# A ConvNeXt V2 block on one core: the slot's conv in two stretches, seven gelu tiles, and work moved between ScalarE, VectorE, GpSimd and TensorE

## The chip, the core and the metric

The kernel runs on one core of a Trainium2 chip. The engines are named as in the profile: PE (TensorE, with its weight loads as PEld), ACT (ScalarE), DVE (VectorE), POOL (GpSimd) and SP (SyncE, which here only issues transfers). Each has a queue of its own that it works off in order. The metric is device time in microseconds (us). Before the change it was 1480.13 us, the median of 3 runs (1479.71 to 1490.58). A difference under about 1% (14.8 us) is treated as one that a measurement of this kernel can't tell from none.

## What is computed

```python
def reference(x, dw, w1, w2, grn_gamma, grn_beta):   # x: 1 x 512 x 512 x 96, bf16
    xp = jnp.pad(x, ((0,0),(1,1),(1,1),(0,0)))
    out = sum(xp[:, i:i+H, j:j+W, :] * dw[i, j] for i in range(3) for j in range(3))
    h = (out - mean(out)) / sqrt(var(out) + 1e-5)      # over the 96 channels
    h = gelu(einsum('bhwc,ce->bhwe', h, w1))           # 96 -> 384, tanh approximation
    gx = sqrt((h * h).sum(axis=(1, 2)) + 1e-6)         # over the whole image
    nx = gx / (gx.mean(axis=-1) + 1e-6)
    h = grn_gamma * (h * nx) + grn_beta + h
    return x + einsum('bhwe,ec->bhwc', h, w2)
```

The sum `gx` runs over the whole image, so nothing can be written before all of `h` has been seen once.

## The kernel before, in words

The image is cut into 128 blocks of 4 rows (2048 pixels). A first pass computes the conv, the norm, the first matrix product and gelu for each block, and from the gelu output only the 384 sums of squares; a few blocks' gelu outputs are kept. A second pass, about the last third of the time, loads or recomputes `h`, multiplies it with `w2` (scaled by the sums) and adds `x`. The change is in the first pass.

The first pass is a loop over slots `s` (line 831). A table `at` (lines 799 to 825) says which block's step of which kind falls into which slot, and within a slot the order of the calls is the order in each engine's queue (`InOrder`). A block `b` passes through these steps:

- `load_x` (SP) and `turn_x` (DVE, two transposes of 128 x 576), three and more slots ahead of the conv.
- The conv, `conv_taps` (lines 462 to 504): 72 matmuls of 64 x 32 weights over 511 or 512 columns. `h` is the half of the array's rows (channels and rows of the input), `j` the output row (a column tile of 32), `i` one of the three PSUM banks of `Y3` (banks 4 to 6), `dx` the horizontal shift; eight tiles (two `h` times four `j`) work side by side. It goes in three bursts of 24 (`taps[0]` to `taps[2]`). In burst `n` the half `h` writes bank `(n + h) % 3`, so that the two halves never write one bank at the same time; `pe.drain()` keeps bursts apart where nothing else lies between.
- `evac`: ACT copies the three banks to `y_bf` (128 x 1536, bf16) in one instruction.
- `stage_sq` one slot later: POOL squares `y_bf`. `stage_stats` two slots after the conv: 24 matmuls with four columns add up `y` and `y * y` over the channels in bank 7 (`S`), up to 64 columns for each of the two sums in a batch of four blocks.
- For a batch: `stage_moments` (DVE: `S / C` from PSUM, then a memset of `S`), one slot later `stage_rstd` (POOL: variance and the integer guess of its inverse root, four small ops), then `stage_newton` (POOL, eight), `stage_turn` (DVE), `stage_rows` and `stage_bcast` (SP, through DRAM). Then for each block `stage_norm` (POOL: `yn = y * rstd`), `stage_write` and `stage_read` (SP, through DRAM), which gives `ynT`.
- `mlp_units(b)`, 14 slots after the conv in the long middle stage: the matrix product with `w1p` in PSUM and gelu on ACT. The block has 12 banks of product. `unit(bank, n)` makes `n` of them and one gelu over them; `banks(2)` gives banks 0 and 1, `banks(1)` banks 2 and 3 in turn. There are nine units: three of two banks and six of one.

The sums of squares come by two ways. A block has four quarters of 512 pixels. For the first `cm_quads(b)` of them (channels on the partitions) DVE runs `bn_stats`, three per quarter (`entry`, called by `squares` and `squares_rest`; the last three of a whole block are owed to the next slot). For the others (pixels on the partitions) PE adds up a Gram matrix, `gram_next(n)`, `n` groups of 6 matmuls of 128 x 128; a quarter is two groups, and groups wait in the list `grams`. Whole blocks (`q % 10` in 0, 3, 7: kept in DRAM for the second pass) have four quarters on DVE, three residues of ten have two, and the other four have three: 90 `bn_stats` and 20 groups in ten slots. The `g` tiles have five buffers.

A slot that has both a conv and an MLP block runs, in this order (lines 895 to 928): `conv(0)`, units 0 and 2, `squares(0)`, `conv(1)`, `turn_x`, units 3 and 4, `squares(1)`, a Gram group, units 6 and 7, `squares(2)`, `turn`, `conv(2)`, `evac`, a Gram group, units 8 and 10, stats, unit 11, moments, the rest of the squares. Slots 18 to 127 are of this kind. Before them slots with a conv alone fill the pipeline, and 14 slots with an MLP block alone (`mlp_tail`) follow.

Of the kernel before, what the change touches and what calls it, by code (L numbers as in the profile page):

```python
# [8 lines left out]
ALU = mybir.AluOpType  # L9
ACTF = mybir.ActivationFunctionType  # L10
AX = mybir.AxisListType

GR = 4
LN_EPS = 1e-5
# [3 lines left out]
BATCH = 4  # L18
NHELD = 5
WHOLE = (0, 3, 7)  # L20
NTAIL = 14
GRB = 3


class InOrder:
# [31 lines left out]
def kernel(  # L57
# [11 lines left out]
    f32 = mybir.dt.float32  # L69
# [30 lines left out]
    def cm_quads(q):  # L100
        if is_whole(q) or is_held(q):
            return NQ
        if q > HELD[0]:
            return 1
        return 2 if q >= NBLK - 16 or (q - 1) % 10 in WHOLE else 3

    whole = [q for q in range(NBLK) if is_whole(q)]
    g_dram = dram.tile([len(whole), 128, NQ * NCH * QW], bf16, name="g_dram")
# [76 lines left out]
    with ExitStack() as p1:  # L185
# [4 lines left out]
        def banks(n):  # L190
            if n == 2:
                return PS[:, 0:2, :]
            ones[0] += 1
            return PS[:, 2 + ones[0] % 2:3 + ones[0] % 2, :]
# [205 lines left out]
        n = 0  # L400
# [61 lines left out]
        def conv_taps(b, spare):  # L462
            if spare:
                Ua, Ub = banks(2), banks(1)
                Y = [Ua[:, 0, :], Ua[:, 1, :], Ub[:, 0, :]]
            else:
                Y = [Y3[:, i, :] for i in range(NI)]
            mms = []
            for n in range(3):
                mms.append([(h, j, (n + h) % NI, dx) for dx in (0, -1, 1) for j in range(GR) for h in range(2)])  # L470
            flat = [m for ms in mms for m in ms]
            first = {}
            last = {}
            for n, (h, j, i, dx) in enumerate(flat):
                first.setdefault((i, j), n)
                last[i, j] = n

            def burst(n, fence=True):
                k = sum(len(ms) for ms in mms[:n])
                for h, j, i, dx in mms[n]:  # L480
                    src = b + shift(h, j)
                    o0, o1 = max(0, -dx), W - max(0, dx)
                    pe.matmul(
                        Y[i][32 * j:32 * j + 32, o0:o1],
                        lhsT=Wq[64 * h:64 * h + 64, i, dx + 1, j, :],
                        rhs=x_rows(src, 64 * h, 64 * h + 64, i, MB * (1 + dx) + o0, o1 - o0)
                        if 0 <= src < NBLK else zrow[64 * h:64 * h + 64, o0:o1],
                        start=first[i, j] == k,
                        stop=last[i, j] == k,
                    )  # L490
                    k += 1
                if n < 2 and fence:
                    pe.drain()

            def evac():
                y = ypool.tile([128, NI, W], bf16, name="y_bf")
                if spare:
                    act.activation(out=y[:, 0:2, :], in_=Ua, func=ACTF.Identity)
                    act.activation(out=y[:, 2, :], in_=Ub[:, 0, :], func=ACTF.Identity)
                else:  # L500
                    act.activation(out=y[:], in_=Y3, func=ACTF.Identity)
                ybf[b] = y

            return [lambda fence=True, n=n: burst(n, fence) for n in range(3)], evac

        def stage_sq(b, on_act):
            q = ysqpool.tile([128, NI, W], bf16, name="ysq")
# [3 lines left out]
                pool.tensor_tensor(out=q[:], in0=ybf[b][:], in1=ybf[b][:], op=ALU.mult)  # L511
            ysq[b] = q

        def stage_stats(b):
            k = batch_of[b]
            b0, n = BATCHES[k]
            for src, h in ((ybf[b], 0), (ysq.pop(b), 1)):
                for g in range(NG):
                    c0 = (b - b0) * NG + g
                    for i in range(NI):  # L520
                        pe.matmul(S[:, h, c0:c0 + (GR - 1) * n * NG + 1:n * NG],
                                  lhsT=src[:, i, g * 128:(g + 1) * 128], rhs=rowsel[:],
                                  start=False, stop=(i == NI - 1), skip_group_check=True)


        def stage_moments(k):
            N = BATCHES[k][1] * GR * NG
            m = small.tile([128, 2, NS], f32, name="mom")
            dve.tensor_scalar(out=m[:, :, :N], in0=S[:, :, :N], scalar1=1.0 / C, scalar2=None, op0=ALU.mult)
            dve.memset(S[:], 0.0)  # L530
            msts[k] = m

        def stage_rstd(k, eng):
            N = BATCHES[k][1] * GR * NG
            m = msts.pop(k)
            var = small.tile([128, NS], f32, name="var")
            eng.tensor_tensor(out=var[:, :N], in0=m[:, 0, :N], in1=m[:, 0, :N], op=ALU.mult)
            eng.tensor_tensor(out=var[:, :N], in0=m[:, 1, :N], in1=var[:, :N], op=ALU.subtract)
            eng.tensor_scalar(out=var[:, :N], in0=var[:, :N], scalar1=0.0, scalar2=LN_EPS, op0=ALU.max, op1=ALU.add)
            ri = small.tile([128, NS], i32, name="ri")  # L540
            eng.tensor_scalar(out=ri[:, :N], in0=var[:, :N].bitcast(i32), scalar1=-0.5, scalar2=float(0x5F3759DF),
                               op0=ALU.mult, op1=ALU.add)
            rcur = ri[:, :N].bitcast(f32)
            rns[k] = (var, rcur)

        def stage_newton(k, eng):
            N = BATCHES[k][1] * GR * NG
            var, rcur = rns[k]
            for it in range(NEWTON_ITERS):
                last = it == NEWTON_ITERS - 1  # L550
                t_ = small.tile([128, NS], f32, name="nt")
                eng.tensor_tensor(out=t_[:, :N], in0=rcur, in1=rcur, op=ALU.mult)
                eng.tensor_tensor(out=t_[:, :N], in0=t_[:, :N], in1=var[:, :N], op=ALU.mult)
                eng.tensor_scalar(out=t_[:, :N], in0=t_[:, :N], scalar1=-0.5, scalar2=1.5, op0=ALU.mult, op1=ALU.add)
                rn = small.tile([128, NS], bf16 if last else f32, name="rstd" if last else "rn")
                if last and N % 32:
                    eng.memset(rn[:, N:(N + 31) // 32 * 32], 0.0)
                eng.tensor_tensor(out=rn[:, :N], in0=t_[:, :N], in1=rcur, op=ALU.mult)
                rcur = rn[:, :N]
            rns[k] = rn  # L560
# [110 lines left out]
        def mlp_tail(b, get):  # L671
# [6 lines left out]
            for t in range(NQ):  # L678
# [11 lines left out]
                        stage_stats(b2)  # L690
                if t > cm_quads(b):
                    grams.extend((b, (t - 1) * QC + k * E) for k in range(0, GR, 2))
            for k in get("moments"):
                stage_moments(k)
            if cm_quads(b) < NQ:
                grams.extend((b, (NQ - 1) * QC + k * E) for k in range(0, GR, 2))

        def mlp_units(b):
# [5 lines left out]
            def cm_mm(dst, j, t):  # L704
                pe.matmul(quad_out(dst), lhsT=w1p[:, j * 128:(j + 1) * 128], rhs=quad(yt[:], t), start=True, stop=True)

            def unit(bank, n):
                U = banks(n)
                if bank < 2 * NCH:
                    j, t0 = divmod(bank, 2)  # L710
                    for t in range(t0, t0 + n):
# [81 lines left out]
        def put(s, what, v):  # L793
            at.setdefault((s, what), []).append(v)
# [4 lines left out]
        for k, (b0, n) in enumerate(BATCHES):  # L799
# [6 lines left out]
            if ramp:  # L806
                put(last_s, "chain", k)
                put(last_s + 1, "spread", k)
            else:
                put(last_s, "moments", k)  # L810
                put(last_s + 1, "rstd", k)
                put(last_s + 2, "newton", k)
                put(last_s + 2, "turn", k)
                put(last_s + 3, "rows", k)
                put(last_s + 4, "bcast", k)
# [15 lines left out]
        for s in range(last_slot + 1):  # L831
# [15 lines left out]
                stage_sq(b, False)  # L847
            for b in get("norm"):
                stage_norm(b)
            for k in get("rstd"):  # L850
                stage_rstd(k, pool)
            mlp = get("mlp")

            def spread_out():
# [11 lines left out]
            elif not mlp:  # L866
                if s + 3 < NBLK:
                    turn_x(s + 3)
                for f in taps:
                    f()  # L870
                if not spare:
                    spread_out()
# [3 lines left out]
                    stage_sq(b, True)  # L876
                for b in get("stats"):
                    stage_stats(b)
                for k in get("moments"):
                    stage_moments(k)  # L880
                if spare:
                    spread_out()
                for k in get("chain"):
# [6 lines left out]
            else:  # L890
                b = mlp[0]
                unit, squares, squares_rest = mlp_units(b)
                conv = lambda n, fence=True: taps[n](fence) if taps else None

                conv(0)
                unit(0, 2)
                unit(2, 1)
                squares(0)
                conv(1, False)
                spread_out()  # L900
                if s + 3 < NBLK:
                    turn_x(s + 3)
                unit(3, 1)
                unit(4, 2)
                squares(1)
                gram_next(1 if taps else 2)
                unit(6, 1)
                squares(2)
                unit(7, 1)
                for k in get("turn"):  # L910
                    stage_turn(k)
                conv(2)
                if evac:
                    evac()
                gram_next(1 if taps else 2)
                unit(8, 2)
                unit(10, 1)
                for b2 in get("stats"):
                    stage_stats(b2)
                unit(11, 1)  # L920
                for k in get("moments"):
                    stage_moments(k)
                squares_rest(2)
                square_owed()
                if is_whole(b):
# [131 lines left out]
```

## Time and profile before

The profiled execution has a span of 1483.2 us; the median of the runs is 1480.13. Busy time is the share of the span in which an engine had an instruction running:

| engine | busy us | share | instructions |
|---|---|---|---|
| PE (matmul) | 1392.2 | 94% | 23125 |
| ACT | 1415.9 | 95% | 1595 |
| POOL | 1300.7 | 88% | 922 |
| DVE | 1166.9 | 79% | 2139 |

These are averages over two passes with different limits. From 300 to 900 us, inside the first pass, the largest groups are (mean length of one, which includes overlap with its neighbours):

| engine | group | count | mean ns |
|---|---|---|---|
| DVE | `bn_stats` 128x512 | 763 | 672 |
| DVE | transposes of x, f32 and bf16 | 79 each | 764 and 736 |
| ACT | gelu 128x512 | 494 | 703 |
| ACT | gelu 128x1024 | 247 | 1118 |
| ACT | `y_bf` 128x1536 | 83 | 1569 |
| POOL | `yn` 128x1536 | 85 | 3111 |
| POOL | `ysq` 128x1536 | 84 | 2754 |
| PE | `w1p` product, 512 columns | 759 | 381 |
| PE | conv, 511 or 512 columns | 5895 | 382 to 394 |
| PE | Gram 128x128 | 1059 | 220 |

In the prediction, "PE PS" and "ACT g" are a matmul into PSUM and a gelu; `g` is the gelu output, `bst` the result of `bn_stats`, `mom`, `var` and `ri` the small tiles of the variance, `o_sb` an output tile of the second pass. Line numbers in the views are those of the helper `InOrder`, so groups are told apart by their tiles.

### The profile page before, as it was taken

Reading aid. Unit: us, or ns where it says so; the run is one execution under the profiler, and the core shown is the slowest. Engines: PE = TensorE matmul, PEld = TensorE weight load, DVE = VectorE, ACT = ScalarE, POOL = GpSimd, SP = SyncE. Lnnn points to the kernel's source line nnn. Section 1 sums busy time; section 2 is a strip of 40 time slices with the busy share of each in tenths; the row PEclk is TensorE's granted clock in tenths of the full one; section 3 lists DMA queues with packets and bytes.
Section 4 is the critical chain, followed back from the end, with each engine's and each line's share of the span. In section 5 each row is a group of like instructions: output and inputs, shape, how many; then the busy total and the mean of one; then the engine's idle time right before and its main releaser. Section 6 shows DMA issues by size and latency. Waiting matters only on the chain.

```text
span 1483.2 us, 54230 instructions
## 1 busy us (share of the span) xinstructions
PE 1392.2 (94%) x23125; PEld 812.3 (55%) x23125; DVE 1166.9 (79%) x2139; ACT 1415.9 (95%) x1595; POOL 1300.7 (88%) x922
## 2 busy tenths in 40 slices
PE   8889999999999999999999997789999999999998
PEld 3334444444444444444444445467777777676766
DVE  7749989999999999999999987955555555555555
ACT  6889999999999999999999999989999999998997
POOL 3459889998999999999999996559999999999997
PEclk9999999999999999999999999999999999999999
DMA  6577788887878888888888867569999999999997
GB/s 178 166 215 235 231 245 282 250 267 243 276 240 274 258 266 259 276 248 280 265 248 264 260 217 210 188 248 404 366 352 410 415 414 413 415 408 410 401 406 279
DMA packets 167768, 433.08 MB, mean 292 GB/s; under 512 B 31558, under 2 KB 81318, under 8 KB 163046
## 3 DMA queue, kind: packets, MB, share of 16 engines
q1 hardware_dynamic: 151284, 326.04, 66.8%
q0 software_dynamic: 14880, 103.43, 17.6%
q8 instruction: 181, 2.97, 0.9%
q14 instruction: 61, 0.50, 0.1%
q10 hardware_dynamic: 1362, 0.15, 0.1%
HBM read 273.30 MB, written 156.22 MB: 290 GB/s over the span
## 4 chain that ended last, share of the span: by engine, by line
PE 31%; ACT 25%; DMA 20%; DVE 10%; POOL 8%; issue 4%; SPq 3%; ACTq 0%; POOLq 0%; DVEq 0%
PE PS L35 31%; ACT g L35 18%; DMA out_dram<-o_sb 9%; ACT y_bf L35 6%; DVE bst L35 5%; POOL yn L35 4%; DMA ynT<-yn_dram 4%; SPq L35 3%; DMA rbc<-r_dram 2%; DMA xin<-in_x_dram 2%; DVE xT L35 2%; DMA yn_dram<-yn 2%; POOL ysq L35 1%; DVE o_sb L35 1%; DMA g_dram<-g 1%
## 5 line engine op out<-in xcount | busy, mean ns | idle before, releaser
L35 ACT ACTIVATE g<-PS 128x512 bf16<-128x512 f32 (+2 forms) x1062 | 727.2, 862 | 9.3 <-PE PS L35 9.1
L35 DVE BATCH_NORM_STATS2 bst<-g 128x6 f32<-128x512 bf16 x1110 | 671.3, 673 | 29.3 <-ACT g L35 28.8
L35 PE MATMUL PS<-ynT,w1p 128*128 128x512 bf16 x2181 | 610.0, 381 | 24.2 <-ACT g L35 5.4
L35 ACT ACTIVATE gr<-PS 128x1536 bf16<-128x1536 f32 x360 | 498.9, 1455 | 27.2 <-PE PS L35 18.7
L35 DVE TENSOR_TENSOR o_sb<-PS,xb 128x384 bf16<-128x384 f32 x512 | 278.0, 557 | 231.2 <-PE PS L35 184.9
L35 POOL TENSOR_TENSOR yn<-y_bf,rbc 128x1536 bf16<-128x1536 bf16 x126 | 391.6, 3111 | 75.1 <-DMA rbc<-r_dram 23.5
L325 POOL TENSOR_TENSOR xb<-xr,B2c 128x1536 f32<-128x1536 bf16 x118 | 368.4, 3133 | 7.9 <-DVE o_sb L35 5.5
L35 PE MATMUL PS<-xT,Wq 64*32 64x511 bf16 (+1 forms) x9198 | 339.7, 388 | 27.5 <-ACT y_bf L35 7.7
L35 POOL TENSOR_TENSOR ysq<-y_bf 128x1536 bf16<-128x1536 bf16 x114 | 314.0, 2755 | 14.4 <-ACT y_bf L35 14.3
L35 PEld LDWEIGHTS <-w1p 128*128 128x128 bf16 x2181 | 171.4, 98 | 221.3 <-issue 130.4
L35 PEld LDWEIGHTS <-gr 128*128 128x128 bf16 x4296 | 213.1, 98 | 75.8 <-issue 19.7
L35 PE MATMUL PS<-W2s,gr 128*128 128x96 bf16 x4224 | 224.5, 206 | 13.8 <-DVE o_sb L35 13.4
L35 PEld LDWEIGHTS <-Wq 64*32 64x32 bf16 x9216 | 112.5, 90 | 192.9 <-issue 145.9
L35 ACT ACTIVATE y_bf<-PS 128x1536 bf16<-128x1536 f32 (+2 forms) x135 | 199.4, 1483 | 17.9 <-PE PS L35 13.3
L35 DVE STREAM_TRANSPOSE xT<-xin 128x576 f32<-128x576 f32 (+1 forms) x256 | 181.8, 750 | 13.1 <-DMA xin<-in_x_dram 11.0
L35 PEld LDWEIGHTS <-g 128*128 128x128 bf16 x1704 | 105.1, 98 | 89.1 <-issue 57.4
L35 PE MATMUL PS<-w1p,ynT 128*128 128x256 bf16 (+2 forms) x822 | 125.6, 273 | 7.7 <-ACT xT L35 3.2
L35 PE MATMUL PS<-g 128*128 128x128 bf16 x1464 | 122.9, 220 | 5.0 <-DVE PS L35 4.9
L35 PEld LDWEIGHTS <-gl 128*128 128x128 bf16 x1680 | 82.9, 98 | 24.4 <-issue 2.4
L35 PE MATMUL PS<-W2s,gl 128*128 128x96 bf16 x1680 | 89.6, 206 | 1.1 <-DVE o_sb L35 0.8
L35 PEld LDWEIGHTS <-ynT 128*128 128x128 bf16 x822 | 64.1, 98 | 31.1 <-issue 13.3
L280 POOL DMA_DIRECT2D xr<-in_x_dram x115 | 63.8, 555 | 14.2 <-POOL xb L325 14.2
(106 smaller groups left out, 559.9 us busy)
## 6 DMA issues: line engine op xcount, KB each, us to landing
xin<-in_x_dram SPq DMA_DIRECT2D x126, 432.0 KB
g_dram<-g SPq DMA_DIRECT2D x105, 512.0 KB
gl<-g_dram POOLq DMA_DIRECT2D x35, 1536.0 KB, 10.9
yn_dram<-yn SPq DMA_DIRECT2D x512, 96.0 KB
ynT<-yn_dram SPq DMA_DIRECT2D x128, 384.0 KB
out_dram<-o_sb SPq DMA_DIRECT2D x127, 384.0 KB
xr<-in_x_dram POOLq DMA_DIRECT2D x123, 384.0 KB, 6.9
ynT<-yn_dram SPq DMA_DIRECT2D x85, 512.0 KB
```

The lines of the kernel that those rows point to most:

```text
L35: r = f(*a, **k)
L280: pq.dma_start(out=xr[:], in_=x[0, r0:r0 + GR].rearrange("r w c -> (r w) c").rearrange("(p g) c -> p g c", g=PXP))
L325: pq.tensor_tensor(out=xb[:], in0=grp[q]["xr"][:], in1=bias[:, None, :].to_broadcast([128, PXP, C]), op=ALU.add)
```

## The change

The conv gets a new order, `ROUNDS`: nine rounds of eight matmuls, in which the two halves `h` are always in different banks, cut after 40 matmuls (`SPLIT`) into two stretches. There is no drain inside a slot; where a half enters a bank that the other half has left in the same stretch, a `nop` on PE waits for the other's last matmul there. The MLP has seven units, with fixed places in banks 0 to 3: 0, 2, 6, 8 and 10 of two banks, 4 and 5 of one. The order of the slot changes: units 0 and 2, `conv(0)`, units 4 to 10 with stats and Gram groups between, `conv(1)`, a Gram group, `evac`, variance, the rest of the squares. In the slots whose MLP block ends in 1, 2, 4, 5, 8 or 9 (`FEW`), DVE evacuates bank 0 of the conv and ACT the other two; these blocks now have two quarters on DVE, so ten slots have 81 `bn_stats` and up to three Gram groups per slot (26 are made in ten). The variance and the guess of its root are computed by DVE from PSUM in one go, `stage_moments` stays only for the first batches, and the scaling by `C` moves into `stage_newton`.

```diff
 WHOLE = (0, 3, 7)
+FEW = (1, 2, 4, 5, 8, 9)
 NTAIL = 14
 GRB = 3
+SPLIT = 40
+ROUNDS = ((0, 0, 0, 1, 1, 1, 2, 2, 2), (1, 1, 2, 2, 2, 0, 0, 0, 1))
 
...
-        return 2 if q >= NBLK - 16 or (q - 1) % 10 in WHOLE else 3
+        return 2 if q >= NBLK - 16 or q % 10 in FEW else 3
...
-            mms = []
-            for n in range(3):
-                mms.append([(h, j, (n + h) % NI, dx) for dx in (0, -1, 1) for j in range(GR) for h in range(2)])
-            flat = [m for ms in mms for m in ms]
+            flat = []
+            for n in range(len(ROUNDS[0])):
+                now = [(ROUNDS[h][n], (0, -1, 1)[ROUNDS[h][:n].count(ROUNDS[h][n])]) for h in range(2)]
+                flat += [(h, j) + now[h] for j in range(GR) for h in range(2)]
+            cuts = [0, SPLIT, len(flat)]
...
-            def burst(n, fence=True):
-                k = sum(len(ms) for ms in mms[:n])
-                for h, j, i, dx in mms[n]:
+            enters, mms = {}, {}
+            for n in range(2):
+                left = {}
+                for k in range(cuts[n], cuts[n + 1]):
+                    h, j, i, dx = flat[k]
+                    if j == 0 and (i, 1 - h) in left:
+                        enters[k] = left.pop((i, 1 - h))
+                    if j == GR - 1:
+                        left[i, h] = k
+
+            def burst(n):
+                for k in range(cuts[n], cuts[n + 1]):
+                    h, j, i, dx = flat[k]
+                    if k in enters:
+                        hold = pe.nop()
+                        tc.add_manual_dep(hold.ins, mms[enters[k]].ins.name,
+                                          mybir.DependencyInfo(mybir.DependencyClass.Sync, mybir.DependencyReason.DATA),
+                                          reason="row tiles of one bank")
                     src = b + shift(h, j)
...
-                    pe.matmul(
+                    mm = pe.matmul(
...
                         stop=last[i, j] == k,
                     )
-                    k += 1
-                if n < 2 and fence:
-                    pe.drain()
-
-            def evac():
+                    mms[k] = mm
+
+            def evac(split=False):
...
                     act.activation(out=y[:, 2, :], in_=Ub[:, 0, :], func=ACTF.Identity)
+                elif split:
+                    dve.tensor_copy(out=y[:, 0, :], in_=Y3[:, 0, :])
+                    act.activation(out=y[:, 1:3, :], in_=Y3[:, 1:3, :], func=ACTF.Identity)
                 else:
                     act.activation(out=y[:], in_=Y3, func=ACTF.Identity)
...
-            return [lambda fence=True, n=n: burst(n, fence) for n in range(3)], evac
+            return [lambda n=n: burst(n) for n in range(2)], evac
...
-        def stage_stats(b):
+        def stage_stats(b, *hs):
             k = batch_of[b]
             b0, n = BATCHES[k]
-            for src, h in ((ybf[b], 0), (ysq.pop(b), 1)):
+            for h in hs or (0, 1):
+                src = ysq.pop(b) if h else ybf[b]
...
-        def stage_rstd(k, eng):
+        def stage_rstd(k):
             N = BATCHES[k][1] * GR * NG
-            m = msts.pop(k)
+            neg = small.tile([128, NS], f32, name="neg")
+            dve.tensor_scalar(out=neg[:, :N], in0=S[:, 0, :N], scalar1=-1.0 / C, scalar2=None, op0=ALU.mult)
+            dve.tensor_tensor(out=neg[:, :N], in0=S[:, 0, :N], in1=neg[:, :N], op=ALU.mult)
             var = small.tile([128, NS], f32, name="var")
-            eng.tensor_tensor(out=var[:, :N], in0=m[:, 0, :N], in1=m[:, 0, :N], op=ALU.mult)
-            eng.tensor_tensor(out=var[:, :N], in0=m[:, 1, :N], in1=var[:, :N], op=ALU.subtract)
-            eng.tensor_scalar(out=var[:, :N], in0=var[:, :N], scalar1=0.0, scalar2=LN_EPS, op0=ALU.max, op1=ALU.add)
+            dve.tensor_tensor(out=var[:, :N], in0=S[:, 1, :N], in1=neg[:, :N], op=ALU.add)
+            dve.memset(S[:], 0.0)
+            dve.tensor_scalar(out=var[:, :N], in0=var[:, :N], scalar1=0.0, scalar2=C * LN_EPS,
+                              op0=ALU.max, op1=ALU.add)
             ri = small.tile([128, NS], i32, name="ri")
-            eng.tensor_scalar(out=ri[:, :N], in0=var[:, :N].bitcast(i32), scalar1=-0.5, scalar2=float(0x5F3759DF),
-                               op0=ALU.mult, op1=ALU.add)
-            rcur = ri[:, :N].bitcast(f32)
-            rns[k] = (var, rcur)
+            dve.tensor_scalar(out=ri[:, :N], in0=var[:, :N].bitcast(i32), scalar1=-0.5,
+                              scalar2=float(0x5F3759DF), op0=ALU.mult, op1=ALU.add)
+            rns[k] = (var, ri[:, :N].bitcast(f32))
...
-                eng.tensor_scalar(out=t_[:, :N], in0=t_[:, :N], scalar1=-0.5, scalar2=1.5, op0=ALU.mult, op1=ALU.add)
+                f = C ** 0.5 if last else 1.0
+                eng.tensor_scalar(out=t_[:, :N], in0=t_[:, :N], scalar1=-0.5 * f, scalar2=1.5 * f,
+                                  op0=ALU.mult, op1=ALU.add)
...
-            def unit(bank, n):
-                U = banks(n)
+            def unit(bank, n, at):
+                U = PS[:, at:at + n, :]
...
             else:
-                put(last_s, "moments", k)
-                put(last_s + 1, "rstd", k)
+                put(last_s, "rstd", k)
...
                 stage_norm(b)
-            for k in get("rstd"):
-                stage_rstd(k, pool)
...
-                for f in taps:
+                for n, f in enumerate(taps):
+                    if n:
+                        pe.drain()
                     f()
...
-                for k in get("moments"):
-                    stage_moments(k)
+                for k in get("rstd"):
+                    stage_rstd(k)
...
@@ -890,36 +914,36 @@
             else:
                 b = mlp[0]
                 unit, squares, squares_rest = mlp_units(b)
-                conv = lambda n, fence=True: taps[n](fence) if taps else None
-
+                conv = lambda n: taps[n]() if taps else None
+
+                unit(0, 2, 0)
+                unit(2, 2, 2)
+                squares(0)
                 conv(0)
-                unit(0, 2)
-                unit(2, 1)
-                squares(0)
-                conv(1, False)
                 spread_out()
                 if s + 3 < NBLK:
                     turn_x(s + 3)
-                unit(3, 1)
-                unit(4, 2)
+                unit(4, 1, 0)
+                for b2 in get("stats"):
+                    stage_stats(b2, 0)
+                unit(5, 1, 1)
                 squares(1)
-                gram_next(1 if taps else 2)
-                unit(6, 1)
+                unit(6, 2, 2)
                 squares(2)
-                unit(7, 1)
+                for b2 in get("stats"):
+                    stage_stats(b2, 1)
+                gram_next(1)
                 for k in get("turn"):
                     stage_turn(k)
-                conv(2)
+                unit(8, 2, 0)
+                gram_next(1)
+                unit(10, 2, 2)
+                conv(1)
+                gram_next(1)
                 if evac:
-                    evac()
-                gram_next(1 if taps else 2)
-                unit(8, 2)
-                unit(10, 1)
-                for b2 in get("stats"):
-                    stage_stats(b2)
-                unit(11, 1)
-                for k in get("moments"):
-                    stage_moments(k)
+                    evac(b % 10 in FEW)
+                for k in get("rstd"):
+                    stage_rstd(k)
                 squares_rest(2)
                 square_owed()
                 if is_whole(b):
```

More of the change, by code (lines that the diff above doesn't have):

```diff
@@ L902 @@
                     turn_x(s + 3)
-                unit(3, 1)
-                unit(4, 2)
+                unit(4, 1, 0)
+                for b2 in get("stats"):
+                    stage_stats(b2, 0)
+                unit(5, 1, 1)
                 squares(1)
-                gram_next(1 if taps else 2)
-                unit(6, 1)
+                unit(6, 2, 2)
                 squares(2)
-                unit(7, 1)
+                for b2 in get("stats"):
+                    stage_stats(b2, 1)
+                gram_next(1)
                 for k in get("turn"):
                     stage_turn(k)
-                conv(2)
-                if evac:
-                    evac()
-                gram_next(1 if taps else 2)
-                unit(8, 2)
-                unit(10, 1)
-                for b2 in get("stats"):
-                    stage_stats(b2)
-                unit(11, 1)
-                for k in get("moments"):
-                    stage_moments(k)
+                unit(8, 2, 0)
[3 more added lines that the diff above has]
+                gram_next(1)
+                if evac:
+                    evac(b % 10 in FEW)
+                for k in get("rstd"):
+                    stage_rstd(k)
                 squares_rest(2)
```

## The prediction, made before the changed kernel had run

> **What bounds the kernel now.** I began with the windows, to see which engine is full and where. These are ten slots of the long middle stage (columns: window, its length, then the busy time of PE, weight loads, DVE, ACT and POOL with counts, the granted clock, the DMA share):
>
> ```profile
> core 0: us, PE busy (x) PEld busy (x) DVE busy (x) ACT busy (x) POOL busy (x), PEclk, DMA share, GB/s
> 500.00:570.50 70.50, 67.97 (x1246) 33.38 (x1230) 68.37 (x122) 70.50 (x101) 66.46 (x52) 1.00 0.87 273
> ```
>
> A slot lasts 7.05 us. ACT has no idle time, but PE, DVE and POOL stand at 94 to 97%: relief for one engine is worth only the distance to the next. The clock is full and stays out of the sum. Then the chain of waits in order of time, one slot of it (start, length, what):
>
> ```profile
> 513.58 0.88 PE PS L35 x16
> 514.45 0.12 issue
> 514.57 0.36 PE PS L35
> 514.93 3.74 ACT g L35 x6
> 518.67 0.33 issue
> 519.00 1.57 ACT y_bf L35
> 520.57 0.04 issue
> ```
>
> It closes on itself: `conv(0)` (0.88 and the drain's 0.12), the first MLP unit (0.36), six gelus with their start (4.07), the evacuation `y_bf` (1.57 and 0.04), and then `conv(0)` may write the banks again: 7.04 us, the whole slot. The loop is `evac -> conv(0) -> unit 0 -> gelus -> evac`, and DVE and POOL are not in it.
>
> For prices I took the timeline, where the distance between two starts is what an instruction costs its engine (recorded lengths overlap):
>
> ```profile
> 510.10 1.10 ACT L35 ACTIVATE g<-PS 128x1024 bf16<-128x1024 f32 x1
> 511.01 0.68 ACT L35 ACTIVATE g<-PS 128x512 bf16<-128x512 f32 x1
> 511.96 1.56 ACT L35 ACTIVATE y_bf<-PS 128x1536 bf16<-128x1536 f32 x1
> 513.29 5.92 ACT L35 ACTIVATE g<-PS 128x1024 bf16<-128x1024 f32 x9
> 515.32 0.88 PE L35 MATMUL PS<-xT,Wq 64*32 64x512 bf16 x24
> 516.13 0.85 PE L35 MATMUL PS<-ynT,w1p 128*128 128x512 bf16 x3
> 501.99 3.00 DVE L35 BATCH_NORM_STATS2 bst<-g 128x6 f32<-128x512 bf16 x5
> 1100.52 0.56 DVE L35 TENSOR_TENSOR o_sb<-PS,xb 128x384 bf16<-128x384 f32 x1 [0.54 <-PE PS L35]
> 16.57 0.17 DVE L35 TENSOR_SCALAR var<-var 128x16 f32<-128x16 f32 x1
> 16.78 0.18 DVE L35 TENSOR_SCALAR ri<-var 128x16 int32<-128x16 int32 x1
> ```
>
> ACT: a two-bank gelu 0.91 (510.10 to 511.01), a one-bank gelu 0.475 (two of them from 511.01 to 511.96), a three-bank evacuation 1.33 (511.96 to 513.29). PE: a burst of 24 conv matmuls without a drain 0.81 (515.32 to 516.13), with one 0.99 (513.58 to 514.57 in the chain). DVE: a `bn_stats` 0.585 ((3.00 - 0.67) / 4); a small op that waits for the one before it 0.21 at 16 columns.
>
> **The change, per slot.** 110 slots hold both a conv and an MLP block (18 to 127: from slot 18 the MLP block is slot - 14, and convs end at 127), so 0.01 us per slot is 1.1 us.
>
> *ACT.* Now 3 x 0.91 + 6 x 0.475 + 1.33 = 6.91. Seven tiles: 5 x 0.91 + 2 x 0.475 = 5.50; the merging alone saves 0.08. The evacuation is 1.33 in 4 slots of ten and, with two banks, 0.91 in 6. Sum 6.83 or 6.41, mean 6.58: 0.33 less. This is no gain by itself, for ACT then waits for others.
>
> *DVE.* Nine `bn_stats` fewer in ten slots (90 to 81, from `cm_quads`): -9 x 0.585 = -5.3. Six copies of one bank from PSUM more: no row has a copy. Below it is the `bn_stats` step of the same 512 columns (0.585), above it the `o_sb` row from PSUM at its full length and 128 columns longer (0.56 x 512 / 384 = 0.75); I take 0.61, nearer the step, because steps overlap: +3.7. The variance: now `mom` and `memset`, 0.28 + 0.17 (from their group rows 275 and 165 ns); then five dependent ops of 64 columns and a `memset`. The 16-column step is 0.21; 48 columns more cost up to 0.05 (at the `bn_stats` rate, 0.585 / 512 each) and reading PSUM may add, so 5 x 0.24 + 0.07 (a `memset`'s 0.17 less the overlap) = 1.27, bounds 1.05 and 1.5: +0.8 for each batch of four blocks, 2.5 batches in ten slots, +2.0. DVE's 68.4 becomes 68.8: 6.88 per slot. DVE gets no relief at all.
>
> The Trainium skill, "VectorE: DVE Perf Modes", section "Rules for kernel authors", speaks against moving a chain of small ops here: the flush comes after every op, so count ops. By its fixed part of about 150 cycles (and 8 of fill) a 64-column op would be an estimated 0.23 us on its own and six of them 1.39, which would put 0.03 us more on a slot and 3 us on the total. The 0.21 step of the ramp's chain agrees with the rule.
>
> *POOL.* Four ops a batch go (0.30 + 0.32 + 0.43 + 0.24 = 1.29): 0.32 per slot less of 6.65. POOL's square now waits for a later evacuation, with `norm` behind it in its queue, and behind that SP's `write` with `rows`, the `g` stores and the next x load in the same queue; they have 1 to 4 slots of lead, so I put 0. If that cover failed, the 2.75 of a square would show once per slot.
>
> *PE.* Three bursts cost 0.99 + 0.81 + 0.81 = 2.61. 72 matmuls are nine rounds of eight; a round is 0.216 (a 512-column matmul's step), so a burst is 3 x 0.216 + 0.16, and two stretches are 1.94 + 0.32 = 2.26. Two waits on PE's own matmuls replace the drain; nothing like them is in the trace. The one in `conv(0)` holds round four for the last matmul of round two, which ends (0.28 + 0.38) just as round four is due (3 x 0.216): 0 to 0.2 (a drain costs 0.18), I take 0.1. The one in `conv(1)` looks three rounds back: 0. More Gram work: 26 against 20 groups in ten slots at 0.35 each (518.49 to 518.84 in the timeline), +0.2. Net 0. The stats matmuls move, they don't grow. The conv-only slots trade two drains for one and the waits: 0.
>
> *The loop.* The evacuation stands last, so the loop becomes: evacuation of two banks (1.57 - 0.43 = 1.14) + 0.04; `conv(0)` of 40 matmuls, 0.81 + 2 x 0.216 + 0.1 = 1.34; unit 4 to its gelu, 0.46 (unit 0's second matmul starts at 514.80, its gelu at 515.26); gelus 4 and 5, 0.95; gelu 6 to its end, 1.10 + 0.05, because unit 10 needs its banks; unit 10, 0.43 + 0.09; `conv(1)` of 32, 0.88 + 0.22, and 0.10 to ACT (a conv-only slot's conv ends at 70.53, its evacuation starts at 70.62). Sum 6.80; in the four slots with three banks 7.23; mean 6.97. After a stall ACT starts empty, and in the ramp such evacuations last 1.02 and 1.45: 0.12 less, 6.85. I take 6.91, the middle. Inside it ACT stands idle before gelu 4 (0.3) and before the evacuation (0.15).
>
> *The new wait.* The copy stands in DVE's queue ahead of the variance, the remaining `bn_stats` and the next slot's, and behind this slot's first six and the two transposes; `conv(0)` of the next slot waits for it, and all PE behind that. After MLP blocks ending in 1, 4 and 8 DVE holds 3 x 0.585 left over from a whole block + 6 x 0.585 + 1.34 (transposes) + 0.61 = 7.2 between two copies, against 6.80 of the loop. `rstd` adds 1.27 in five slots of twenty. The next slot's stats on PE wait for its `memset`, 3 us after the evacuation began; that is covered unless the copy is 2 us late. A copy may be about 0.4 late (it takes 0.7 of the evacuation's 1.14) before it costs anything. So the wait is between nothing and 0.25 per slot (0.4 in three of ten, 1.2 in one, nothing taken off); I take 0.1, since intervals after 2, 5 and 9 hold only 5.5 and give lateness back. Slot: 7.01.
>
> **Rivals.** *Forecast:* DVE takes ACT's place; 7.05 to 7.01 is -4 us: 1476. For it: the DVE sum, which hardly moves. Chance 0.48, good for 1465 to 1495 (7.18 to 6.92 per slot).
>
> *Copies never late:* then the slot is the larger of DVE's 6.88 and the loop's 6.85: -0.17 x 110 = -19, 1461. For it: DVE is idle only 3% now, and the light and heavy slots alternate. Against: any idle DVE time is lost, for the squares of a slot cannot start before its first gelu has ended, some 2 us after the evacuation began (0.91 + 1.1). Chance 0.27.
>
> *The copy holds PE (other side):* the loop at its upper 6.97 and the wait at 0.25: 7.22, +0.17 x 110 = +19, 1499. It decides as soon as copies end more than 0.4 after ACT's half of the evacuation. For it: DVE's 7.2 against 6.80. Chance 0.25. If also the waits in the conv cost 0.2 and not 0.1, 11 us more.
>
> **The numbers.** The profiled run's 1483.2 is 0.2% over the median 1480.13; the sum is a difference, laid on the median. Within 1% is 1465.3 to 1494.9, about what such a measurement can tell from no change. Faster 0.25 (nearly all of the second case), same 0.51, slower 0.24. Range: from 1457, DVE at its lower bounds (6.81, and the loop 6.85 with it), to 1503, the third case with a third of those 11 us; a tenth is left out at each end.
>
> **What would show it.** Slot length between evacuations: 7.01, 6.88 or 7.22. ACT's windows should fall to some 94%, DVE's rise to 97% or more; the copy's step 0.61; `rstd` 1.27 a batch; two conv stretches of 1.34 and 1.0 on PE. If PE sits idle until a DVE copy before most `conv(0)`, the third case holds; if DVE has idle time ended by gelus and ACT is full, the loop was priced too low. I am wrong if the time moves while the slots between 120 and 880 us stay at 7.05.

## The result, and the profile after

The changed kernel takes 1583.26 us (median of 4 runs, 1579.25 to 1587.27): 1.0673 times the kernel before (1481.64 here, the median of 4 runs), 95% interval 1.0643 to 1.0703. That is 100 us slower, outside the range, and no rival had priced it. The profiled execution's span is 1580.7.

The same window as before (same columns):

```profile
500.00:570.50 70.50, 61.73 (x1126) 33.11 (x1104) 67.66 (x109) 62.75 (x72) 55.57 (x34) 0.96 0.70 212
```

ACT, full before, now has 8 us of idle time, POOL 15, PE 9. Only DVE is as busy as it was, but with less than nine slots in the window instead of ten. The granted clock, full before, is 0.96. The evacuations show where the time went: most slots last 6.7 to 7.5 us, near the forecast, but in three of five batches one slot lasts 12 to 16. The chain of waits in order of time no longer runs through ACT:

```profile
517.72 2.35 DVE bst L38 x4
520.07 0.60 DVE y_bf L38
520.67 0.04 issue
520.72 5.27 PE PS L38 x89
```

What happens there shows in the timelines of DVE and of POOL (start, length, engine, line, operation; in brackets idle time and what ended it):

```profile
520.59 0.21 DVE L38 TENSOR_SCALAR neg<-PS 128x64 f32<-128x64 f32 x1
520.83 0.23 DVE L38 TENSOR_TENSOR neg<-PS,neg 128x64 f32<-128x64 f32 x1
521.09 0.22 DVE L38 TENSOR_TENSOR var<-PS,neg 128x64 f32<-128x64 f32 x1
521.42 0.17 DVE L38 MEMSET PS<- 128x128 f32 x1
521.49 2.14 DVE L38 TENSOR_SCALAR var<-var 128x64 f32<-128x64 f32 x1
523.66 3.03 DVE L38 TENSOR_SCALAR ri<-var 128x64 int32<-128x64 int32 x1
```

```profile
520.83 2.75 POOL L38 TENSOR_TENSOR ysq<-y_bf 128x1536 bf16<-128x1536 bf16 x1 [1.26 <-DVE neg L38]
523.54 3.10 POOL L38 TENSOR_TENSOR yn<-y_bf,rbc 128x1536 bf16<-128x1536 bf16 x1
```

Two ops on 64 columns take 2.14 and 3.03 us, ten times the others and more. The first ends at 523.63, POOL's square at 523.58; the second at 526.69, POOL's norm at 526.64. Over the long stage 33 of the 56 such ops take over 0.4 us, and each of them ends 47 to 54 ns after a POOL instruction. Those that start while POOL is idle take 0.19. The view by tile, between 100 and 1010 us (lengths in ns, min/median/max):

```profile
L38 DVE TENSOR_TENSOR var<-PS,neg x28: 224/224/226, 135.9 to 1002.7; 128x64 f32<-128x64 f32 x28
L38 DVE TENSOR_SCALAR var<-var x28: 184/2143/2722, 136.3 to 1003.1; 128x64 f32<-128x64 f32 x28
L38 DVE TENSOR_SCALAR ri<-var x28: 195/3022/3036, 137.2 to 1003.4; 128x64 int32<-128x64 int32 x28
```

No view of waits lists this: the record counts it as the op's own length and DVE as busy. Taken over 0.19 each, the 56 ops are 80.7 us too long.

What PE waits for shows how the loss reaches the slot. From 300 to 900 us, first in the changed kernel, then in a version with the old variance (e3 below):

```profile
PE PS L38 <- DVE y_bf L38: 73.1, 31, 7.2
```

```profile
PE PS L38 <- DVE y_bf L38: 16.5, 30, 1.6
```

The number of waits is about the same, but single ones now last up to 7.2 us. After the two long ops DVE works through its queue with hardly a pause and reaches the next copy late: behind the batch shown above at 544.94, when ACT had begun its own part of that evacuation at 540.69. The clock adds to it. Between 120 and 880 us PE waited 13 times for 4.1 to 7.2 us before `conv(0)`, for example here:

```profile
535.09 1.39 PE L38 MATMUL PS<-xT,Wq 64*32 64x512 bf16 x40 [0.34 <-ACT y_bf L38]
545.66 2.02 PE L38 MATMUL PS<-xT,Wq 64*32 64x512 bf16 x40 [4.15 <-DVE y_bf L38]
```

The granted clock is 1.00 from 541.5 to 545.6 us and 0.62 from 545.6 to 547.6. After each of the 13 gaps `conv(0)` took 1.95 to 2.27 us up to the next matmul, against 1.30 to 1.35 after 19 gaps of 0.5 to 1.8 us, and the next evacuation began 7.5 us after the start of `conv(0)` on average, not 5.7: some 23 us for the 13, on top of the waits.

### The profile page after: what moved, and what is told of

It reads as the page before. It is cut to its first block, busy times and chain, and to the rows that moved or that the text cites. A ratio compares the mean times of both kernels' runs of the same rounds, so it can differ in the third digit from the quotient of the medians.

```text
span 1580.7 us, 54880 instructions
## 1 busy us (share of the span) xinstructions
PE 1412.2 (89%) x23620; PEld 861.8 (55%) x23620; DVE 1254.0 (79%) x2228; ACT 1402.2 (89%) x1367; POOL 1263.9 (80%) x798
## 4 chain that ended last, share of the span: by engine, by line
PE 42%; DVE 27%; DMA 13%; ACT 7%; issue 4%; POOL 4%; SPq 2%; ACTq 0%; DVEq 0%; POOLq 0%
PE PS L38 42%; DVE bst L38 16%; DMA out_dram<-o_sb 7%; ACT g L38 4%; DVE xT L38 4%; POOL yn L38 4%; DMA ynT<-yn_dram 3%; DMA yn_dram<-yn 2%; DVE y_bf L38 2%; SPq L38 2%; ACT y_bf L38 2%; DVE var L38 1%; DVE ri L38 1%; ACT xT L38 1%; DVE o_sb L38 1%
## 5 line engine op out<-in xcount | busy, mean ns | idle before, releaser
L38 ACT ACTIVATE g<-PS 128x1024 bf16<-128x1024 f32 (+1 forms) x834 | 721.2, 931 | 127.6 <-PE PS L38 125.9
L38 DVE BATCH_NORM_STATS2 bst<-g 128x6 f32<-128x512 bf16 x1011 | 618.5, 673 | 57.1 <-ACT g L38 56.6
L38 PE MATMUL PS<-ynT,w1p 128*128 128x512 bf16 x2082 | 591.5, 384 | 16.5 <-ACT g L38 6.2
L38 PEld LDWEIGHTS <-Wq 64*32 64x32 bf16 x9216 | 119.8, 91 | 301.7 <-issue 213.5
L38 ACT ACTIVATE y_bf<-PS 128x1024 bf16<-128x1024 f32 (+2 forms) x135 | 157.1, 1169 | 16.4 <-PE PS L38 16.4
L38 PE MATMUL PS<-w1p,ynT 128*128 128x384 bf16 (+2 forms) x1020 | 156.1, 277 | 10.4 <-ACT g L38 4.1
L38 PE MATMUL PS<-g 128*128 128x128 bf16 x1860 | 156.7, 221 | 2.2 <-DVE PS L38 2.2
L38 PEld LDWEIGHTS <-g 128*128 128x128 bf16 x2100 | 125.9, 98 | 54.5 <-issue 35.9
L38 PEld LDWEIGHTS <-ynT 128*128 128x128 bf16 x1020 | 88.2, 99 | 42.0 <-issue 20.5
```

The source lines that it names most:

```text
L38: r = f(*a, **k)
```

## The experiments

Ratios are to the kernel before on the same chip, with 95% intervals.

**e1_two_inputs.** The two ops get a second input from SBUF (code shortened here and below):

```diff
-dve.tensor_scalar(out=var, in0=var, scalar1=0.0, scalar2=C * LN_EPS, op0=ALU.max, op1=ALU.add)
+dve.scalar_tensor_tensor(out=var, in0=var, scalar=0.0, in1=k_eps.to_broadcast([128, N]), op0=ALU.max, op1=ALU.add)
```

(likewise the guess `ri`, with the constant `k_magic`).

> The changed kernel, with the two long DVE ops of the variance (the clamp var<-var and the guess ri<-var, both tensor_scalar from SBUF to SBUF) written as scalar_tensor_tensor with a broadcast constant as second SBUF input; the values are the same. In the changed kernel these two take up to 3.0 us instead of 0.19 and end 47 to 54 ns after a POOL instruction ends; their excess adds up to 80.7 us over 28 batches. Theory A (these ops hold still while POOL runs, because a one-input op from SBUF to SBUF uses a second port that POOL holds; an op with two inputs does not wait): both at 0.19 to 0.25, total about 1583 - 81 = 1502, slots of a variance back at 7 to 8 us. Theory A' (any DVE op that reads SBUF through a second port waits, two-input ops included): as the changed kernel, 1570 to 1595. Rival B (the loss is the copy that holds PE, or the conv's new waits; the long ops only fill time in which DVE would wait anyway): 1570 to 1595, with the two ops short and idle time in their place.

1571.75, 1.0593 (1.0556 to 1.063). The form of the op changes little: 30 of the 56 ops are still long, 74.8 us in all. The guess still ends just behind POOL's instruction (norm from 525.15, 3.11 long, to 528.26):

```profile
523.10 2.17 DVE L38 SCALAR_TENSOR_TENSOR var<-var,k_eps 128x64 f32<-128x64 f32 x1
525.30 3.04 DVE L38 SCALAR_TENSOR_TENSOR ri<-var,k_magic 128x64 int32<-128x64 int32 x1
```

Theory A falls and A' holds. The time does not tell rival B apart, though it had all these ops short.

**e2_from_psum.** The same `tensor_scalar` ops, but their source stays in PSUM:

```diff
-dve.tensor_tensor(out=var, in0=S[:, 1], in1=neg, op=ALU.add)
-dve.memset(S, 0.0)
-dve.tensor_scalar(out=var, in0=var, ...)
+dve.tensor_tensor(out=S[:, 1], in0=S[:, 1], in1=neg, op=ALU.add)
+dve.tensor_scalar(out=S[:, 0], in0=S[:, 1], ...)
+dve.tensor_scalar(out=var, in0=S[:, 1], ...)
 ...
-dve.tensor_scalar(out=ri, in0=var, ...)
+dve.tensor_scalar(out=ri, in0=S[:, 0], ...)
+dve.memset(S, 0.0)
```

> The changed kernel, with the same tensor_scalar ops, but reading PSUM: the variance is formed in place in S, and clamp and guess read it from there (one small op more per batch). Theories A and A' both say that an op with a PSUM source does not wait for POOL: all variance ops at 0.18 to 0.33, total 1495 to 1510 (1583 - 81, less or more by the 31 extra ops of 0.2). Rival B: 1570 to 1595 as the changed kernel.

1495.67, 1.0089 (1.0057 to 1.0121): 88 us gone, 86 by the ratios. What changed is the place of an operand (with it one op more, and the `memset` comes last). Between 100 and 1010 us all 56 ops take 0.21 to 0.22, and 34 of them lie wholly inside a POOL instruction. DVE's timeline, while POOL's square runs from 507.33 to 510.08:

```profile
508.12 0.22 DVE L38 TENSOR_SCALAR var<-PS 128x64 f32<-128x64 f32 x1
508.26 0.21 DVE L38 TENSOR_SCALAR ri<-PS 128x64 int32<-128x64 int32 x1
```

Rival B falls: copy, conv order and waits are still there.

**e3_undo_variance.** The variance part undone (`moments` on DVE, four ops on POOL a slot later), the rest of the change kept.

> The changed kernel with the variance back as it was: moments on DVE, the four small ops on POOL one slot later. Theory A: the 81 us go, and DVE is 0.8 us per batch lighter than with the ops on it: 1480 to 1500; what remains over the kernel before is the price of the other parts (copy, conv order, seven tiles, Gram). Rival B: 1565 or more.

1484.64, 1.0011 (0.9985 to 1.0037): all other parts together change nothing that can be measured. Against e2 it is 11 us less: so much the longer work of the variance on DVE costs, with e2's added op, where no op waits for POOL.

**e4_variance_alone.** The kernel before with the variance part alone.

> The kernel before with only the variance part of the change (six DVE ops from PSUM at the end of the slot instead of two, the four POOL ops gone). Theory A: the two ops wait here too for a POOL instruction that runs, 2 to 5 us per batch of 31; DVE has 0.2 us per slot to spare, so the total goes up by 60 to 120: 1540 to 1600. Rival B: 1475 to 1490, as before, since DVE gains only 0.8 us per batch and no copy or new conv is there.

1515.01, 1.0223 (1.0159 to 1.0287). The ops wait here as well, 47.8 us in all, but the total rises by only 31, below the range expected, and a part of that is the longer work. There is no copy for PE to wait for, but the late DVE holds PE at another place: the Gram sums lie in the bank of `S`, and a Gram group waits for the `memset` of `S`. From 300 to 900 us, first e4, then the kernel before:

```profile
PE PS L35 <- DVE PS L35: 31.1, 18, 3.5
```

```profile
PE PS L35 <- DVE PS L35: 3.6, 6, 1.2
```

That the rest of the wait went into DVE's idle time is likely, but not shown.

**d1_copy_sbuf, d2_memset_sbuf.** One DVE op per batch added to e2 that nobody needs:

```diff
+dve.tensor_copy(out=spare_, in_=ident_b[:, 0:64])     # d1: SBUF to SBUF
+dve.memset(spare_, 0.0)                               # d2, in its place
```

> e2_from_psum (1495.7, no variance op waits) with one more DVE op per batch behind the variance: a copy of 64 bf16 columns from SBUF to SBUF, of a constant, whose result nobody reads. Theory A' (any DVE op that takes a second SBUF port waits until POOL's running instruction ends, whatever the op and whoever needs it): the copy takes 0.1 to 0.2 us where POOL is idle and up to 3.0 where it runs, and the total goes up by 20 to 60 us, 1515 to 1555. Rival F (only the chain var to guess waits, because each op reads what the one before has just written): the copy takes under 0.2 us everywhere, 1493 to 1499.

> e2_from_psum with a memset of 64 bf16 columns of SBUF in the place of that copy. It reads nothing. If the wait is for a read through a second port (A'), it takes under 0.2 us everywhere and the total stays at 1493 to 1500; if it is for the writing side as well, it waits like the copy: 1515 to 1555.

d1: 1558.12, 1.0515 (1.0484 to 1.0546); d2: 1496.91, 1.011 (1.0078 to 1.0142). By tile, first d1, then d2:

```profile
L38 DVE COPY spare<-ident_b x28: 171/1662/2435, 134.8 to 974.7; 128x64 bf16<-128x64 bf16 x28
```

```profile
L38 DVE MEMSET spare<- x28: 85/85/85, 132.5 to 915.8; 128x32 uint32 x28
```

Rival F falls: a copy of a constant waits too, 26 of 28 times. Its 45.4 us over 0.19 each cost 62 in total, a little over the range expected: it stands ahead of the `bn_stats`, and these ahead of the next slot's copy, for which PE waits 3.3 to 4.1 us in twelve slots. After ten of these waits `conv(0)` took 1.80 to 2.27, as in the changed kernel. A `memset` of SBUF does not wait, though 27 of 28 lie wholly inside a POOL instruction.

**e5_no_copy, c1_copy_always, c2_spread, c3_var_split** ask what limits the rest, from e3 on. e5 has `evac()` in every slot. c1 has `evac(True)` in every slot and 6 in `FEW`. c2 adds the spreading to c1 (and sums up a block's results two slots after its MLP):

```diff
-squares_rest(2)
-square_owed()
+if owed: owed.pop(0)()
 if is_whole(b):
-    owed.append(lambda f=squares_rest: f(3))
+    some(0)                                            # two bn_stats now
+    owed.extend(lambda k=k, f=some: f(k) for k in (1, 2))   # two in each of the next slots
```

c3 takes the first three ops and the `memset` of the changed kernel's `stage_rstd` in place of `moments`, and leaves clamp and guess to POOL.

> The changed kernel with the variance undone (1484.6, slots of 6.72 to 7.2) and without the DVE copy: ACT evacuates three banks in every slot. Theory C (a slot is the loop evacuation, conv(0), gelus 4 to 6, unit 10, conv(1): 6.75 with two banks on ACT, 7.18 with three, plus what a late copy adds): all slots at 7.15 to 7.2, total 1484.6 + (7.18 - 7.07) x 110 = 1494 to 1500. Rival D (DVE, not the loop, sets the slots of 7.0 to 7.2; the copy costs more than it brings): 1470 to 1480, as DVE loses 0.36 us per slot.

> The changed kernel with the variance undone, and DVE copies one bank in every slot with a conv and an MLP block; the blocks ending in 6 have two quarters on DVE like those in FEW, so ten slots have 78 bn_stats and 28 Gram groups. Theory C: no slot of 7.18 is left, but after whole blocks and the slots behind them DVE holds 7.2 between two copies, so 6.9 to 7.0 on average: 1466 to 1477. Rival D: 1485 to 1495, for DVE gets 0.24 us of copies more per slot and 0.18 of bn_stats less.

> c1_copy_always with the six late bn_stats of a whole block spread by two over its slot and the next two, instead of three and three. Theory C: DVE holds 6.6 or less between two copies, under the loop's 6.75: 6.75 to 6.85, 1452 to 1463. Rival E (POOL binds next: a square of 2.71, a norm of 3.05, and twelve small ops per batch, 4.9 / 4, make 6.98 by their steps): 6.95 to 7.0, 1470 to 1476. Rival D: as c1.

> c2_spread with the variance split between DVE and POOL: DVE forms it from PSUM in three ops and clears S (0.3 us per batch more than now), POOL keeps only clamp and guess (two ops less, 0.2 us per slot). No DVE op reads and writes SBUF with one input or two. Theory C: as c2 or 1 to 5 us more, DVE being 0.08 per slot heavier. Rival E: 0.15 per slot better than c2: 1452 to 1460.

| kernel | us | ratio | 95% interval |
|---|---|---|---|
| e5_no_copy | 1490.00 | 1.0048 | 1.0029 to 1.0067 |
| c1_copy_always | 1487.56 | 1.0026 | 1.0003 to 1.0049 |
| c2_spread | 1485.01 | 1.002 | 1.0002 to 1.0039 |
| c3_var_split | 1468.42 | 0.9918 | 0.989 to 0.9945 |

In e5 the evacuations of three banks follow at 7.16 and 7.19 (ACT's timeline; the median from 120 to 880 us is 7.18):

```profile
505.76 1.45 ACT L38 ACTIVATE y_bf<-PS 128x1536 bf16<-128x1536 f32 x1
512.92 1.45 ACT L38 ACTIVATE y_bf<-PS 128x1536 bf16<-128x1536 f32 x1
520.11 1.45 ACT L38 ACTIVATE y_bf<-PS 128x1536 bf16<-128x1536 f32 x1
```

So the loop of theory C is real, though the total stays 4 us under its range. Rival D's gain without the copy (1470 to 1480) did not come; against e3 the two intervals overlap. c1 and c2 shorten half of the slots and more to 6.7 to 6.8, but the totals stay: theory C missed by 11 us in c1 and by 22 in c2, and both totals lie where rival D put them. In both, some slots of 7.5 to 10.6 remain. c3 speaks for rival E: with two POOL ops fewer per batch it is 16.6 us faster than c2, although DVE, which rival D holds to be the limit, has more to do (windows of c2, then of c3, columns as above):

```profile
300.00:800.00 500.00, 480.42 (x9155) 266.76 (x9152) 477.91 (x843) 480.65 (x568) 472.82 (x355) 1.00 0.85 263
```

```profile
300.00:800.00 500.00, 482.96 (x9221) 267.58 (x9220) 488.45 (x888) 484.50 (x573) 467.77 (x324) 1.00 0.85 265
```

So POOL was most likely the next limit, at a busy share of 95%. In c2's window POOL has the least waiting of the four engines, 11 us of 500 (PE, ACT and DVE 18 to 20); the rest of its idle time lies between its small ops. Rival E's totals were still some 9 us too low, in c2 as in c3. c3 is the only version here whose interval lies under 1, by 0.8%, less than the 1% that counts as a difference here, and DVE, at 98%, is likely its limit.

## Why the prediction was wrong

*The step that failed* is the price of the variance on DVE, "5 x 0.24 + 0.07 = 1.27, bounds 1.05 and 1.5". The 0.21 step came from the ramp's chain, and there POOL was idle. In the long stage, where POOL was at 94% before the change, clamp and guess took 2.9 us more per batch on average (80.7 / 28). The whole variance, from `neg` to the next op, took 4.15 instead of 1.27: 1.24 in the best batch, 6.62 in the worst. The bounds missed it because both ends came from rows without the condition that matters, what POOL does at the same time. e2, with the operand in PSUM, has the price I had put: 508.65 - 507.08 = 1.57 for seven ops, 1.30 without the added one. So the 100 us are, by the ratios of the runs, some 86 for the ops that stood still, some 12 for the longer work of the variance on DVE (e2 against e3), and nothing measurable for the rest.

What the runs show is that an op of the kinds tried (`tensor_scalar`, `scalar_tensor_tensor`, copy) with its source in SBUF stands still while a POOL instruction runs; that a port is behind it is the explanation of the Trainium skill, which I had not weighed. Its page "SBUF — State Buffer", section "Who interferes with whom", says that DVE has one pair of SBUF ports of its own and one shared with GpSimd, that a copy or `tensor_scalar` in a 2-port mode, or an op with two SBUF inputs against a GpSimd instruction that reads SBUF, needs the shared one, and that whoever comes first keeps it for the whole instruction. The trace agrees in every point that was tried: ends at 47 to 54 ns behind POOL's (35 to 40 in d1, about 80 in e1), one-input and two-input ops alike, none with a PSUM source. Three two-input ops of e1 began 0.07 to 0.13 us after a square of POOL's and stayed at 0.21; these three squares are the longest of 110, 2.83 to 2.89 against 2.75, as if there POOL had waited. By this rule the price would have been an estimated rest of a POOL instruction per op, up to 2.75 or 3.1 us. I weighed another rule of the skill, on the number of ops, and its 0.03 us per slot was no part of the loss.

*The other prices held.* `conv(0)` takes 1.34 (506.95 to 508.29 in PE's timeline; put at 1.34), `conv(1)` 1.03 (511.40 to 512.43; put at 1.0), which fits the 0.1 that I had taken for the waits that replaced the drain. The copy's step is 0.59 (512.74 to 513.33; put at 0.61). The loop is 6.72 to 6.78 with two banks and 7.1 to 7.2 with three, against 6.80 and 7.23.

*DVE gets no relief* was right. Only e2 can show it, because in the changed kernel the ops that stand still count as busy: from 300 to 800 us DVE is busy 477.2 us there for 69 evacuations, 6.92 each (484.6 for 71 before, 6.83). e2 has 7.17 as its median slot, near the 7.22 of the third case and over the forecast's 7.01. The late copy costs nearer to 0.25 than to 0.1 there. Without the ops that stood still the forecast would still have missed by 17 to 20 us (1495.67, or 1.0089 times 1480, against 1476), one added op included, but within its range.

*POOL at 0* held for this kernel: e2, with the four ops gone from POOL, is slower than e3, which has them. But "0.32 per slot less" is not worthless everywhere: c2 against c3 points to POOL as the limit once DVE is relieved. Its small ops keep 0.08 us between them, which the busy share leaves out.

*The third rival* had the side, not the mechanism: PE does sit idle before `conv(0)` until a copy, but most of it, 73.1 us against 16.5 with the old variance, comes from two ops of the batch before, not from `bn_stats`. That the clock would drop behind long waits was in no case of the forecast, which left the clock out of the sum.

## What to carry to other kernels

Before a small op is moved to DVE, look at what POOL does at that moment: an op that copies or scales from SBUF to SBUF, or has two SBUF inputs, stood still until POOL's instruction had ended, and the profile shows that as the op's own length. Keep its source in PSUM, or leave it on POOL. A price from a row holds only with the neighbours that the row had. When engines stand within 5% of each other, each must be summed by the steps between its starts, gaps included.

## What was not expected of the hardware

A 64-column op took 0.19 us or up to 3.03, depending on what POOL did (56 ops of the changed kernel). The same `tensor_scalar` from PSUM took 0.21 to 0.22 during POOL's square. The `memset` of SBUF and `bn_stats`, with one input or none, showed no such length (85 ns each of 28; 0.67 us). The total rose by 0.65 of the time that ops stood still in e4, by 1.37 of it in d1: what such a wait costs depends on what stands behind it in the queue, and on the clock. PE's granted clock fell to 0.62 behind a gap of 4.15 us, and in the changed kernel `conv(0)` was slow behind all 13 gaps of 4.1 us and more and behind none of 19 gaps of 0.5 to 1.8 us.
